# A fused FFT mixer and two MLPs: two blocks' MLP in halves by turns, fewer weight conversions in the first transform's columns, banks dealt by use

## The chip, the cores and the metric

The kernel runs on one core of a Trainium2 chip. The metric is the device time of one execution in microseconds, as the median of several runs. The kernel before took 1379.32 us (three runs, 1379.2 to 1383.39).

## What is computed

The input is x of shape 4 x 3136 x 256 (batch, sequence, channels). Three layers follow one another:

```python
X = np.fft.rfft(x, axis=1)
y = np.fft.irfft(X * (filt_r + 1j * filt_i), n=3136, axis=1)
h = y.transpose(0, 2, 1) @ U @ V
u = y + h.transpose(0, 2, 1)
u = u + np.maximum(u @ w_ch1, 0) @ w_ch2
xn = (u - mean(u)) / sqrt(var(u) + 1e-6) * g_ln
out = u + np.maximum(xn @ w_ch1b, 0) @ w_ch2b
```

The ranks and widths are 32 (U, V) and 1024 (both MLPs). U, V and the four weights arrive in 64-bit floating point and are converted on the chip; most products are made from two 32-bit pieces, a high and a low one.

## The kernel before, in words

**Head.** Batch 0's transform is done first and alone. `First.rows` (L431) multiplies the rows, `First.columns` (L500) works through 14 pairs of columns, numbered j = 0 to 13, with a tail of three more turns (`BACKL` = 3). One turn j of the columns does, for different columns at once: four transposes `psz` on TensorE (L538), their copy `z` on ACT (L546), the product `ps2` (L555) of the column before, the filter (`filt`, L218: two copies `psx` of crossed halves on ACT, the multiplications L228 and L231 on VectorE, the sum L232 on POOL), the product `ps3` (L564) of the column three turns back with a slot of `d` that holds the inverse matrix and that column's piece of U, and the copies of the result (`spill` L520, `project` L528). U's piece is copied into its slot by POOL (L574, L577), `UAHEAD` = 1 turn ahead. The PSUM pools are `ps_h` (three banks), `ps_o` (four) and `ps_t` (one). Before the change `psz` and both `ps3` share the four banks of `ps_o`, and the crossed halves of odd columns lie in `ps_t`.

**The converter.** `stagger` (L826) runs 18 jobs, each one piece of a weight or of V: job n starts at slot 4n, its two ACT conversions (L807, L808) come in that slot, then one VectorE instruction per slot (L794, L796, L798, L800), POOL's L812 and L814, the high piece (`keep`, mostly ACT) at slot 4n + 8 and the low piece (`last`, L885) in the next. Each `next(pr)` runs one slot. `ROWSLOTS` and `COLSLOTS` say how many slots go into which row and column; the main loop runs two slots per step until the jobs are done. A job's data are fetched to a staging tile some jobs ahead, by SP.

**Main loop.** The tokens lie in blocks of 512. A step (L1016) is one eighth of a block's MLP: the first product `psh` (`m1`, L663), ACT's and VectorE's halves `hh` and `hl` (L674, L675), and, two steps later, the second product `pso` (`m2`, L679). Phases are (a, k) for MLP 1 of block k and (b, k) for MLP 2, in the order a0 a1 a2 b0 b1 a3 b2 a4 b3 a5 and so on, eight steps each. `end` (L701) closes a phase: for MLP 1 it forms the tile `x2` (L712, L718, L721) and stores it (L750), for MLP 2 it adds and stores the output (L732, L742). A unit (L636) makes 448 tokens from the transform's last stage; its two loads (L628 and L634, `load_unit`) are issued on SP one unit ahead, and only if its batch's transform is complete. A block's units are due at steps 3 and 6 of the phase that `ahead` names. Batches 1 to 3 are transformed beside the loop by the generator `rest`: from step `FFT0` on, `RATE` pieces per step. `Spectrum.finish` (L273) completes a batch. All engines' queues run in the order in which the program is written.

Of the kernel before, what the change touches and what calls it, by code (L numbers as in the profile page):

```python
# [10 lines left out]
F32 = mybir.dt.float32  # L11
# [9 lines left out]
P = 128  # L21
PP, NM, NG = 112, 28, 28
KT, FT = D // P, FF // P
# [11 lines left out]
AHEAD = 3  # L35
FETCHES = (1, 2, 5, 6)

SLOTS, UAHEAD = 8, 1
PACE = 4
ROWSLOTS = (1, 2, 2, 2, 3, 3, 3, 4, 5, 5, 6, 6)  # L40
COLSLOTS = (0, 1, 1, 2, 2, 3, 3, 4, 4, 5, 5, 6, 6) + tuple(range(7, 14))
VSTEP = 9
DIRECT = 4

PARTS, UPARTS = (0, 1, 2, 5, 6, 8), 10
LEAD = 3
FFT0, RATE = 23, 0.75

XTURN, XREAD, XSTAT, XROOT = (3, 4), 8, (10, 11), 12
BW = 32  # L50
# [90 lines left out]
def fft_mixer_kernel(ctx: ExitStack, tc: tile.TileContext, x, U, V, flt, w1, w2, gln, w1b, w2b,  # L141
# [25 lines left out]
    def acopy(o, i, scale=1.0):  # L167
        nc.scalar.activation(out=o, in_=i, func=AF.Copy, scale=scale)  # L168
# [35 lines left out]
    def flat(t):  # L204
        return t.rearrange("p a d -> p (a d)")

    class Spectrum:
# [7 lines left out]
            nc.sync.dma_start(ft, flt[:, 2 * i:2 * i + 2])  # L215
            self.flt[i] = ft

        def filt(self, i, ps, room=None):  # L218
            ft = self.flt.pop(i)
            if room and i % 2:  # L220
                xs, ya = (mp.tile([P, BLK], F32, tag=tag, name=tag, bufs=3).rearrange("p (a d) -> p a d", a=2) for tag in ("hh", "hl"))
            else:
                xs = fp.tile([P, 2, D], F32, tag="xs", name="xs", bufs=2)
                ya = fp.tile([P, 2, D], F32, tag="ya", name="ya", bufs=3)
            crossed = room.tile([P, 512], F32, tag="t" if room is ps_t else "h", name="psx") if room else flat(xs)
            acopy(crossed[0:64], ps[64:128], -1.0)
            acopy(crossed[64:128], ps[0:64])
            nc.vector.tensor_tensor(out=ya, in0=ps.rearrange("p (a d) -> p a d", a=2), in1=ft[:, :, 0], op=ALU.mult)  # L228
            if room:
                def cross():  # L230
                    nc.vector.tensor_tensor(out=xs, in0=crossed.rearrange("p (a d) -> p a d", a=2), in1=ft[:, :, 1], op=ALU.mult)  # L231
                    (nc.gpsimd if i > 1 else nc.vector).tensor_tensor(out=ya, in0=ya, in1=xs, op=ALU.add)  # L232

                self.y[i] = ya, cross if i else cross()
                return
            nc.gpsimd.tensor_tensor(out=xs, in0=xs, in1=ft[:, :, 1], op=ALU.mult)  # L236
            self.y[i] = ya, xs
# [134 lines left out]
    class First:  # L372
# [127 lines left out]
        def columns(self):  # L500


            sp = Spectrum(0, self.flt)
            zt, n, w = {}, NCH, PP + R
            d0, d1 = self.d
            self.t = d1[:, 1, 0:KT * 2 * R].rearrange("p (h g r) -> p h g r", h=KT, g=2)
            turns = [self.u_half(h) for h in (1, 0)]

            def slot(g):
                return d1[:, 0] if g == 0 else d0[:, g % SLOTS]  # L510

            def total(j):
                if ADDL <= j < n + ADDL:
                    cross = sp.y[n - 1 - j + ADDL][1]
                    if cross:
                        cross()

            def spill(pvs, i):
                for dh, pv in enumerate(pvs):
                    (nc.vector.tensor_copy if dh else acopy)(self.big[:, dh, 2 * i * PP:2 * (i + 1) * PP].rearrange("p (g w) -> p g w", w=PP), pv[:, :, :PP])  # L520

            def project(pvs, i):
                for dh, pv in enumerate(pvs):
                    acc = self.t[:, dh]
                    if i == n - 1:
                        nc.vector.tensor_copy(acc, pv[:, :, PP:])
                    else:
                        nc.vector.tensor_tensor(out=acc, in0=pv[:, :, PP:], in1=acc, op=ALU.add)  # L528

            due = None  # L530
            for j in range(n + BACKL):
                if j < n:
                    i = n - 1 - j
                    ps = ps_o.tile([P, 512], F32, tag="o", name="psz")
                    for g in range(2):
                        for dh in range(KT):
                            a = g * D + dh * P
                            nc.tensor.transpose(ps[:PP, a:a + P], self.big[:, dh, (2 * i + g) * PP:(2 * i + g + 1) * PP], ident)  # L538
                total(j)
                if due:  # L540
                    spill(*due)
                    project(*due)
                due = None
                if j < n:
                    zt[i] = wide(F32, "fin", "z0", D, 3)
                    acopy(flat(zt[i]), ps[:PP])  # L546
                if 0 < j <= n:
                    i = n - j
                    z = zt.pop(i)
                    ps = ps_h.tile([P, 512], F32, tag="h", name="ps2")  # L550
                    if i == 0:
                        for g in range(2):
                            nc.tensor.matmul(ps[:, g * D:(g + 1) * D], self.e[:, 1 - g], z[:, g], start=True, stop=True)
                    else:
                        nc.tensor.matmul(ps, self.e[:, 0], flat(z), start=True, stop=True)  # L555
                    sp.filt(i, ps, ps_t if i % 2 else ps_h)
                if j >= BACKL:
                    i = n + BACKL - 1 - j
                    ya = sp.y.pop(i)[0]
                    pvs = []  # L560
                    for dh in range(KT):
                        ps = ps_o.tile([P, 512], F32, tag="o", name="ps3")
                        for g in range(2):
                            nc.tensor.matmul(ps[:, g * w:(g + 1) * w], dealt(ya[:, g], dh), slot(2 * i + g),  # L564
                                             start=True, stop=True)
                        pvs.append(ps[:, :2 * w].rearrange("p (g w) -> p g w", w=w))
                    due = pvs, i
                if j in UTURN:
                    next(turns[UTURN.index(j) // 2], None)
                self.filters(j + AHEAD)  # L570
                if BACKL - UAHEAD <= j < n + BACKL - UAHEAD:
                    i = n + BACKL - UAHEAD - 1 - j
                    for g in () if i else range(2):
                        nc.gpsimd.tensor_copy(slot(g)[:, PP:w], self.uf[:, g])  # L574
                    if i:
                        g = 2 * i % SLOTS
                        nc.gpsimd.tensor_copy(d0[:, g:g + 2, PP:w], self.uf[:, 2 * i:2 * i + 2])  # L577
                yield j
            project(*due)
            spill(*due)  # L580
# [120 lines left out]
    def end(ph):  # L701
# [1 line left out]
        n = blen(k)  # L703
        acc = po.pop(ph)
        if kind == "a":
            x2 = mp.tile([P, BLK // BW, BW, KT], F32, tag="x2", name="x2", bufs=1)

            def cut(t, dh):
                return t[k][:, dh, :n].rearrange("p (j c) -> p j c", c=BW)

            for dh in range(KT):
                nc.vector.tensor_tensor(out=x2[:, :n // BW, :, dh], in0=acc[dh][:, :n].rearrange("p (j c) -> p j c", c=BW),  # L712
                                        in1=f32(cut(acth, dh)), op=ALU.add)
            while len(todo) <= XROOT:
                todo.append([])
            for dh in range(KT):
                o, ah, al = x2[:, :n // BW, :, dh], cut(acth, dh), cut(actl, dh)
                todo[dh].append(lambda o=o, al=al: nc.vector.tensor_tensor(out=o, in0=o, in1=f32(al), op=ALU.add))  # L718
                todo[dh + 1].append(lambda o=o, ah=ah: acopy(ah, o))
                todo[dh + 2].append(lambda o=o, ah=ah, al=al: sub(al, o, f32(ah)))  # L720
                todo[XTURN[dh]].append(lambda o=o: nc.vector.transpose(out=o, in_=o))  # L721
            todo[XTURN[-1]].append(lambda: x2store(k, x2))
            todo[XREAD].append(lambda: x2load(k))
            for j, at in enumerate(XSTAT):
                todo[at].append(lambda j=j: x2stat(k, j))
            todo[XROOT].append(lambda: x2root(k))
            return
# [205 lines left out]
    with tc.manual_schedule():  # L933
# [6 lines left out]
        def chain():  # L940
# [2 lines left out]

        first = First()
        pr = stagger([w_job("w1", w1, 0, "wt"), w_job("w1", w1, 1, "wt"), v_job(0), v_job(1)] + [w_job(nm, w, j) for nm, w, j in (
            ("w2", w2, 0), ("w1", w1, 2), ("w1", w1, 3), ("w2", w2, 1), ("w2", w2, 2),
            ("w2", w2, 3), ("w1b", w1b, 0), ("w1b", w1b, 1), ("w2b", w2b, 0), ("w1b", w1b, 2), ("w1b", w1b, 3),
            ("w2b", w2b, 1), ("w2b", w2b, 2), ("w2b", w2b, 3))])
        first.load(pr)
# [62 lines left out]

        later = leftover()
        units_to(need(0))
        steps = [(ph, f) for ph in phases for f in range(FT)]
        for idx in range(len(steps) + 2):  # L1016
            if idx < len(steps):
                ph, f = steps[idx]
# [56 lines left out]
```

## Time and profile before

| what | value |
|---|---|
| median of three runs | 1379.32 us |
| the profiled execution | 1375.99 us |
| its span | 1374.2 us |
| mean granted TensorE clock | 0.999 |
| TensorE's slices 1 to 3 of 40, in tenths | 8, 7, 8 |
| TensorE's slices 4 to 39 | 9 |
| DMA, mean | 110 GB/s |

A slice is 34 us; 9 stands for 90% or more. "Idle before" in a row is the time in which the engine had nothing to run just before the instruction, with what ended it. Matmuls overlap, so their busy times can add up to more than the time that passes.

### The profile page before, as it was taken

Reading aid. Unit: us, or ns where it says so; the run is one execution under the profiler, and the core shown is the slowest. Engines: PE = TensorE matmul, PEld = TensorE weight load, DVE = VectorE, ACT = ScalarE, POOL = GpSimd, SP = SyncE. Lnnn points to the kernel's source line nnn. Section 1 sums busy time; section 2 is a strip of 40 time slices with the busy share of each in tenths; the row PEclk is TensorE's granted clock in tenths of the full one; section 3 lists DMA queues with packets and bytes.
Section 4 is the critical chain, followed back from the end, with each engine's and each line's share of the span. In section 5 each row is a group of like instructions: output and inputs, shape, how many; then the busy total and the mean of one; then the engine's idle time right before and its main releaser. Section 6 shows DMA issues by size and latency. Waiting matters only on the chain.

```text
span 1374.2 us, 18678 instructions
## 1 busy us (share of the span) xinstructions
PE 1342.1 (98%) x6870; PEld 1118.4 (81%) x6870; DVE 826.4 (60%) x1660; ACT 549.2 (40%) x1019; POOL 170.2 (12%) x173
## 2 busy tenths in 40 slices
PE   8789999999999999999999999999999999999998
PEld 7478788877888888888888888888888888888887
DVE  6878966577545546666555557675455445454554
ACT  4764544466333334554333335553222222222221
POOL 2846601022000001111000001110000000000000
PEclk9999999999999999999999999999999999999999
DMA  9735267474535534533345345443012112210111
GB/s 260 250 89 150 78 154 198 142 204 131 136 96 145 141 80 146 152 115 103 93 118 154 87 126 163 125 140 92 17 50 65 44 34 74 66 20 28 46 47 39
DMA packets 140155, 151.10 MB, mean 110 GB/s; under 512 B 60528, under 2 KB 116160, under 8 KB 139968
## 3 DMA queue, kind: packets, MB, share of 16 engines
q1 hardware_dynamic: 133600, 138.61, 36.1%
q0 software_dynamic: 5888, 10.50, 3.3%
q8 instruction: 54, 0.88, 0.3%
q10 hardware_dynamic: 576, 0.80, 0.2%
q14 instruction: 37, 0.30, 0.1%
HBM read 102.34 MB, written 47.54 MB: 109 GB/s over the span
## 4 chain that ended last, share of the span: by engine, by line
PE 86%; DVE 6%; ACT 2%; DMA 2%; issue 2%; POOL 1%; SPq 0%; DVEq 0%; ACTq 0%; POOLq 0%
PE psh L671 36%; PE pso L698 13%; PE pso L699 6%; PE pso L690 6%; PE pso L691 6%; PE pso L692 6%; PE psu L642 3%; PE ps L200 2%; PE ps L202 2%; PE ps L201 2%; DMA x<-x 1%; ACT xs L168 1%; PE psu L644 1%; DVE hl L675 1%; DVE x2t L732 1%
## 5 line engine op out<-in xcount | busy, mean ns | idle before, releaser
L675 DVE SCALAR_TENSOR_TENSOR hl<-psh,hh 128x512 fp32r<-128x512 f32 (+1 forms) x400 | 270.9, 678 | 411.9 <-ACT hh L674 411.5
L674 ACT ACTIVATE hh<-psh 128x512 fp32r<-128x512 f32 (+1 forms) x400 | 235.1, 588 | 624.8 <-PE psh L671 619.1
L698 PE MATMUL pso<-wb,hh 128*128 128x512 f32 x784 | 285.2, 397 | 0.9 <-DVE x L712 0.8
L671 PE MATMUL psh<-ah,wb 128*128 128x512 f32 (+1 forms) x800 | 276.7, 387 | 0.0
L699 PE MATMUL pso<-wb,hl 128*128 128x256 f32 x784 | 219.9, 280 | 0.6 <-DVE hl L675 0.6
L671 PEld LDWEIGHTS psh<-ah,wb 128*128 128x128 f32 x800 | 149.7, 188 | 33.3
L698 PEld LDWEIGHTS pso<-wb,hh 128*128 128x128 f32 x784 | 147.3, 188 | 35.2 <-DVE x L712 3.2
L690 PE MATMUL pso<-hh,w2h 128*128 128x512 f32 (+1 forms) x400 | 156.2, 390 | 1.0 <-DVE x2t L732 0.9
L691 PE MATMUL pso<-hl,w2h 128*128 128x512 f32 (+1 forms) x400 | 155.1, 388 | 1.6 <-DVE hl L675 1.4
L671 PE MATMUL psh<-ah,w1h 128*128 128x512 f32 (+1 forms) x400 | 155.5, 389 | 0.4 <-DVE hl L675 0.3
L671 PE MATMUL psh<-al,wb 128*128 128x512 f32 (+1 forms) x400 | 155.3, 388 | 0.0
L671 PE MATMUL psh<-al,w1h 128*128 128x512 f32 (+1 forms) x400 | 155.0, 387 | 0.0
L671 PE MATMUL psh<-ah,w1l 128*128 128x512 f32 (+1 forms) x400 | 154.6, 387 | 0.0
L692 PE MATMUL pso<-hh,w2l 128*128 128x512 f32 (+1 forms) x400 | 154.4, 386 | 0.0
L699 PEld LDWEIGHTS pso<-wb,hl 128*128 128x128 f32 x784 | 148.1, 189 | 6.9 <-DVE hl L675 1.2
L236 POOL TENSOR_TENSOR xs<-xs,ft 128x512 f32<-128x512 f32 x42 | 54.3, 1294 | 392.5 <-ACT xs L168 392.5
L690 PEld LDWEIGHTS pso<-hh,w2h 128*128 128x128 f32 x400 | 75.2, 188 | 19.2 <-issue 4.2
L691 PEld LDWEIGHTS pso<-hl,w2h 128*128 128x128 f32 x400 | 75.2, 188 | 17.4 <-DVE hl L675 3.7
L671 PEld LDWEIGHTS psh<-ah,w1h 128*128 128x128 f32 x400 | 75.2, 188 | 16.2 <-DVE hl L675 0.8
L671 PEld LDWEIGHTS psh<-ah,w1l 128*128 128x128 f32 x400 | 75.1, 188 | 15.8
L692 PEld LDWEIGHTS pso<-hh,w2l 128*128 128x128 f32 x400 | 75.1, 188 | 15.3
L671 PEld LDWEIGHTS psh<-al,w1h 128*128 128x128 f32 x400 | 75.3, 188 | 12.5 <-DVE al L171 0.2
(163 smaller groups left out, 1775.8 us busy)
## 6 DMA issues: line engine op xcount, KB each, us to landing
ft<-flt SPq DMA_DIRECT2D x42, 512.0 KB, 4.4
xd<-x SPq DMA_DIRECT2D x96, 128.0 KB, 2.9
x2t<-xd SPq DMA_DIRECT2D x24, 512.0 KB, 4.7
wt<-bd SPq DMA_DIRECT2D x24, 448.0 KB, 5.8
out<-x2t SPq DMA_DIRECT2D x84, 128.0 KB, 2.1
xt<-x SPq DMA_DIRECT2D x42, 224.0 KB, 3.7
zd<-ze SPq DMA_DIRECT2D x42, 224.0 KB, 2.7
zt<-zd SPq DMA_DIRECT2D x42, 224.0 KB, 3.5
```

The source lines that it names most:

```text
L200: nc.tensor.matmul(o, lh, rh, start=True, stop=False)
L201: nc.tensor.matmul(o, lh, rl, start=False, stop=False)
L236: nc.gpsimd.tensor_tensor(out=xs, in0=xs, in1=ft[:, :, 1], op=ALU.mult)
L642: nc.tensor.matmul(ps[:, m:UN:UW], t[:, m, dh * P:(dh + 1) * P], ic[:, m, :], start=m == 0, stop=False, skip_group_check=True)
L671: nc.tensor.matmul(ps[:, :n], w[:, kt, fs], a[:, kt, :n], start=j == 0, stop=j == 3 * KT - 1)
L674: nc.scalar.activation(out=hh[:, :n], in_=ps[:, :n], func=AF.Relu)
L675: nc.vector.scalar_tensor_tensor(out=hl[:, :n], in0=ps[:, :n], scalar=0.0, in1=f32(hh[:, :n]), op0=ALU.max, op1=ALU.subtract)
L690: nc.tensor.matmul(o, wh[:, f, ds], hh[:, :n], start=f == 0, stop=False)
L691: nc.tensor.matmul(o, wh[:, f, ds], hl[:, :n], start=False, stop=False)
L692: nc.tensor.matmul(o, wl[:, f, ds], hh[:, :n], start=False, stop=f == FT - 1)
L698: nc.tensor.matmul(o, hh[:, cs], w, start=f == 0, stop=False, skip_group_check=True)
L699: nc.tensor.matmul(o[:, D:], hl[:, cs], w[:, :D], start=False, stop=f == FT - 1, skip_group_check=True)
```

## The change

- **Converter.** 12 slots in the columns, one in each of columns 0 to 11, and not 20. w2's second piece is converted ahead of w1's second half.
- **Steps.** The first two phases are taken in halves by turns: a0's first four steps, a1's first four, a0's last four, a1's last four. Block 1's `x2` gets a buffer of the tag `x2t`.
- **Columns.** `psz` goes to `ps_t`, all crossed halves to `ps_h`; `ps_o` keeps `ps3`. Odd columns still use the tiles `hh` and `hl`. U's pieces are copied by ACT, two turns ahead. V is loaded at column 11, not 9.
- **Transform of the later batches.** `FFT0` goes from 23 to 25.

```diff
-SLOTS, UAHEAD = 8, 1
+SLOTS, UAHEAD = 8, 2
-COLSLOTS = (0, 1, 1, 2, 2, 3, 3, 4, 4, 5, 5, 6, 6) + tuple(range(7, 14))
-VSTEP = 9
+COLSLOTS = tuple(range(12))
+VSTEP = 11
-FFT0, RATE = 23, 0.75
+FFT0, RATE = 25, 0.75
...
-        def filt(self, i, ps, room=None):
+        def filt(self, i, ps, room=False):
...
-            crossed = room.tile([P, 512], F32, tag="t" if room is ps_t else "h", name="psx") if room else flat(xs)
+            crossed = ps_h.tile([P, 512], F32, tag="h", name="psx") if room else flat(xs)
...
-                    ps = ps_o.tile([P, 512], F32, tag="o", name="psz")
+                    ps = ps_t.tile([P, 512], F32, tag="t", name="psz")
...
-                    sp.filt(i, ps, ps_t if i % 2 else ps_h)
+                    sp.filt(i, ps, True)
...
-                        nc.gpsimd.tensor_copy(slot(g)[:, PP:w], self.uf[:, g])
+                        acopy(slot(g)[:, PP:w], self.uf[:, g])
...
-                        nc.gpsimd.tensor_copy(d0[:, g:g + 2, PP:w], self.uf[:, 2 * i:2 * i + 2])
+                        acopy(d0[:, g:g + 2, PP:w], self.uf[:, 2 * i:2 * i + 2])
...
-            x2 = mp.tile([P, BLK // BW, BW, KT], F32, tag="x2", name="x2", bufs=1)
+            x2 = mp.tile([P, BLK // BW, BW, KT], F32, tag="x2t", name="x2", bufs=2) if k == 1 else \
+                mp.tile([P, BLK // BW, BW, KT], F32, tag="x2", name="x2", bufs=1)
...
-            ("w2", w2, 0), ("w1", w1, 2), ("w1", w1, 3), ("w2", w2, 1), ("w2", w2, 2),
+            ("w2", w2, 0), ("w2", w2, 1), ("w1", w1, 2), ("w1", w1, 3), ("w2", w2, 2),
...
-        steps = [(ph, f) for ph in phases for f in range(FT)]
+        half = FT // 2
+        steps = [(ph, h * half + f) for h in range(2) for ph in phases[:2] for f in range(half)]
+        steps += [(ph, f) for ph in phases[2:] for f in range(FT)]
```

In the changed kernel lines from L707 to L1014 stand one further down (L794 is L795, L732 is L733).

The order of the instructions, first VectorE's in the columns, from the fourth column's first multiplication (`ya`, L228) to the fifth's and past it. Before:

```order
L228 TENSOR_TENSOR ya<-ps_563,f_427 128x512
L798 SCALAR_TENSOR_TENSOR ct<-stg,ct 128x512
L800 TENSOR_SCALAR cyh<-ct 128x512
L231 TENSOR_TENSOR xs<-psx,f_427 128x512
L520 COPY big<-ps_574 128x224
L528 TENSOR_TENSOR d_185<-ps_571,d_185 128x64
L528 TENSOR_TENSOR d_185<-ps_574,d_185 128x64
L228 TENSOR_TENSOR hl<-ps_606,f_456 128x512
L794 TENSOR_SCALAR cyh<-cyh 128x512
L796 TENSOR_SCALAR ct<-cyh 128x512
L231 TENSOR_TENSOR hh<-psx,f_456 128x512
```

And in the changed kernel, the same stretch:

```order
L228 TENSOR_TENSOR ya<-ps_545,f_427 128x512
L801 TENSOR_SCALAR cyh<-ct 128x512
L231 TENSOR_TENSOR xs<-psx,f_427 128x512
L520 COPY big<-ps_556 128x224
L528 TENSOR_TENSOR d_185<-ps_553,d_185 128x64
L528 TENSOR_TENSOR d_185<-ps_556,d_185 128x64
L228 TENSOR_TENSOR hl<-ps_587,f_456 128x512
L795 TENSOR_SCALAR cyh<-cyh 128x512
L231 TENSOR_TENSOR hh<-psx,f_456 128x512
```

Each column now holds one converting instruction, where the early ones held two.

Then SP's queue around the load of batch 1's first unit (`wt<-bd_116`; `bd<-be` are the transform's results, `xd<-x` the store of `x2`, `out<-x2t` block 3's output). Before:

```order
L271 DMA bd_116<-be 112x2x256 x4
L750 DMA xd_94<-x_3441 32x16x64 x4
L628 DMA ic<-c_inv 112x448
L634 DMA wt<-bd_116 112x1024
L742 DMA out<-x2t 32x4x256 x4
L297 DMA xt<-x 112x512 x2
```

And in the changed kernel:

```order
L751 DMA xd_94<-x_3409 32x16x64 x4
L271 DMA bd_116<-be 112x2x256 x2
L743 DMA out<-x2t 32x4x256 x4
L628 DMA ic<-c_inv 112x448
L634 DMA wt<-bd_116 112x1024
L757 DMA x2t<-xd_94 128x4x256
```

The unit's two loads, which stood ahead of the four output stores, stand behind them.

Last VectorE's queue at the same place (`tt` and `tk` are `finish`, `x2t` the eight updates of block 3's output). Before:

```order
L675 SCALAR_TENSOR_TENSOR hl<-psh,hh 128x512
L278 TENSOR_TENSOR tt<-pt,tt 32x256
L171 TENSOR_TENSOR tk<-tt,tk 32x256
L675 SCALAR_TENSOR_TENSOR hl<-psh,hh 128x512 x2
L732 SCALAR_TENSOR_TENSOR x2t<-pso,ln_3309,x2t 128x256 x8
```

And in the changed kernel:

```order
L171 TENSOR_TENSOR yl<-ya,yh 128x512
L675 SCALAR_TENSOR_TENSOR hl<-psh,hh 128x512 x2
L278 TENSOR_TENSOR tt<-pt,tt 32x256
L171 TENSOR_TENSOR tk<-tt,tk 32x256
L733 SCALAR_TENSOR_TENSOR x2t<-pso,ln_3241,x2t 128x256 x8
```

The two instructions of `finish` have moved two steps down, directly ahead of the updates that the stores wait for.

## Rows read from the trace of the kernel before

**Rows 1.** The page, part 1: busy us, share of the span, instructions.

```profile
PE 1342.1 (98%) x6870; PEld 1118.4 (81%) x6870; DVE 826.4 (60%) x1660; ACT 549.2 (40%) x1019; POOL 170.2 (12%) x173
```

**Rows 2.** Windows: stretch, busy time of each engine, clock, DMA share, GB/s.

```profile
31.60:85.90 54.30, 41.62 (x234) 28.82 (x233) 45.32 (x97) 37.36 (x74) 41.09 (x47) 0.97 0.70 216
...
120.00:183.00 63.00, 59.69 (x255) 45.29 (x255) 57.40 (x94) 28.27 (x51) 31.30 (x24) 1.00 0.39 102
```

**Rows 3.** Waits, 48.2 to 81.9 us: us in total, times, longest.

```profile
PE psz L538 <- DVE d L528: 3.4, 2, 2.4
```

**Rows 4.** Groups by line, VectorE, 48.2 to 81.9 us: busy us, mean ns.

```profile
L798 DVE SCALAR_TENSOR_TENSOR ct<-stg,ct 128x512 int32<-128x512 int32 x4 | 3.7, 935 | 0.0
L794 DVE TENSOR_SCALAR cyh<-cyh 128x512 f32<-128x512 f32 x3 | 3.6, 1191 | 0.0
L796 DVE TENSOR_SCALAR ct<-cyh 128x512 int32<-128x512 int32 x3 | 3.5, 1169 | 0.0
...
L800 DVE TENSOR_SCALAR cyh<-ct 128x512 int32<-128x512 int32 x3 | 1.3, 425 | 0.1
```

**Rows 5.** Timeline, VectorE, first columns: start us, us, instruction.

```profile
45.57 0.93 DVE L794 TENSOR_SCALAR cyh<-cyh 128x512 f32<-128x512 f32 x1
46.54 0.60 DVE L796 TENSOR_SCALAR ct<-cyh 128x512 int32<-128x512 int32 x1
```

**Rows 6.** Groups by line, ACT, 48.2 to 81.9 us; last number: idle before.

```profile
L168 ACT ACTIVATE big<-ps 128x224 f32<-128x224 f32 x11 | 3.8, 347 | 1.2 <-PE ps L564 1.1
...
L807 ACT ACTIVATE cyh<-stg 128x512 f32<-128x512 f32 x3 | 2.0, 664 | 0.9 <-ACT vh L168 0.9
```

**Rows 7.** The tile v_sb: first readers, its load, issue to landing.

```profile
L644 PE MATMUL psu<-v_sb,tk x56: 445/451/452, 89.8 to 1240.8; 96*128 96x448 f32 x56
L931 POOL DMA_DIRECT2D v_sb<-vd x1: 548/548/548, 67.5 to 67.5; - x1
...
DMA to landing us min/median/max: 9.9/9.9/9.9
```

**Rows 8.** Groups by line, VectorE, 131 to 180 us (main loop).

```profile
L794 DVE TENSOR_SCALAR cyh<-cyh 128x512 f32<-128x512 f32 x5 | 6.1, 1226 | 0.0
...
L796 DVE TENSOR_SCALAR ct<-cyh 128x512 int32<-128x512 int32 x5 | 4.3, 859 | 0.0
L798 DVE SCALAR_TENSOR_TENSOR ct<-stg,ct 128x512 int32<-128x512 int32 x5 | 3.4, 681 | 0.0
```

**Rows 9.** Timeline, VectorE and then TensorE, steps 26 to 28.

```profile
181.19 1.29 DVE L712 TENSOR_TENSOR x<-pso,ah 128x512 f32<-128x512 f32 x2 [2.39 <-DMA xd<-x]
...
188.81 0.69 DVE L675 SCALAR_TENSOR_TENSOR hl<-psh,hh 128x512 fp32r<-128x512 f32 x1 [1.70 <-ACT hh L674]
...
181.94 0.50 PE L698 MATMUL pso<-wb,hh 128*128 128x512 f32 x1 [0.79 <-DVE x L712]
```

**Rows 10.** Timeline at batch 1's first unit: SP, VectorE, TensorE; then line 634's landing.

```profile
355.18 0.63 SPq L634 DMA_DIRECT2D wt<-bd  x1
362.38 2.75 SPq L742 DMA_DIRECT2D out<-x2t  x4
...
355.53 0.40 DVE L278 TENSOR_TENSOR tt<-pt,tt 32x256 f32<-32x256 f32 x1
356.43 0.41 DVE L171 TENSOR_TENSOR tk<-tt,tk 32x256 fp32r<-32x256 f32 x1 [0.49 <-ACT tk L168]
...
366.71 1.04 PE L642 MATMUL psu<-ic,wt 112*128 112x112 f32 x8
...
DMA to landing us min/median/max: 3.9/5.8/9.8
```

**Rows 11.** Windows of 2 us in the columns, as in rows 2.

```profile
40.00:42.00 2.00, 0.54 (x4) 0.55 (x5) 1.97 (x4) 1.49 (x3) 1.55 (x3) 1.00 0.56 203
42.00:44.00 2.00, 2.00 (x10) 1.64 (x10) 0.86 (x2) 1.62 (x4) 2.00 (x2) 0.57 0.80 199
54.00:56.00 2.00, 0.23 (x2) 0.02 (x1) 1.97 (x3) 1.13 (x3) 1.82 (x2) 1.00 0.88 352
```

## The prediction

> **What bounds the kernel now.** I read the page first: TensorE is busy for 98% of the span and VectorE for 60% [rows 1]. A share like that is an average, so the table of windows comes next. Two stretches at the head stand out [rows 2]; elsewhere TensorE is so full that a change can only make it wait. They are the columns (31.6 to 85.9 us), with TensorE at 41.6 of 54.3 us and VectorE at 45.3, and the stretch of steps 8 to 26 of the main loop (120 to 183 us), with VectorE at 57.4 of 63. In the columns the waits name VectorE: the transposes of the next column waited 3.4 us for the additions that free their bank [rows 3]. So both stretches are paced by VectorE, which converts weights there besides its own work, and a conversion taken out of one comes back in the other.
>
> The page's span is 1374.2 us and the execution that it shows took 1375.99 us; the median of the runs is 1379.32, or 3.33 above. I make the sum against 1375.99 and add 3.33.
>
> **Fewer conversions in the columns.** The order shows what VectorE runs between two columns' first multiplications (L228). From the first column to the fourth there were six conversion instructions and are now three; an L800, an L794 and an L796 are gone, 0.43 + 0.93 + 0.60 = 1.9 us [rows 4, 5]. From the fourth to the last there were thirteen and are now eight: two L798, one L800, one L794, one L796 fewer, 2 x 0.94 + 0.43 + 1.19 + 1.17 = 4.7 us [rows 4]. VectorE paces this stretch, so all of it counts: -6.6 us. If another engine takes over the pace the gain is smaller, down to the 1.9 of the start; if the waits for banks [rows 3] go as well, 3.4 more. I take the middle, as the banks add nothing where VectorE itself is late.
>
> The banks: transposes get the single bank of ps_t, whose last reader is the copy of one column earlier; crossed halves share three banks with the spectra. Every new wait reaches back to work of the column before, so I cost them at 0; what hides them is a column's own 2 to 3 us, and without that cover the price is the 3.4 us again, the other way.
>
> U's copies leave POOL and go to ACT. ACT has none of that form; the nearest is its copy of 224 columns, 0.35 us [rows 6], so 10 columns cost it at most 3.5 us, and no less than nothing. In exchange the stretch loses one pair of ACT's conversions. I cost this at 0 while ACT is not the bound; it is the second rival. The copies stand two columns ahead of their use, so TensorE no longer waits for them. The load of V on POOL moves past two more columns: it was issued at 67.5 us, takes 9.9 to land and is first read at 89.8 [rows 7], so 12.4 us were spare; two columns of at most 3.4 us (from 48.2 to 81.9 us there are ten) leave 5.6, and I cost it at 0.
>
> **What comes back in the loop.** Eight slots of the converter are two weights' worth: two each of L794, L796, L798, L800, 2 x (1.23 + 0.86 + 0.68 + 0.43) = 6.4 us of VectorE [rows 4, 8]. The conversions go on for four steps more, up to step 26. There VectorE was idle for 2.39 and 1.70 us [rows 9], 4.1 us that can take them, which leaves 2.3. The 2.39 was a wait for the store of the tile x2, which held up TensorE by 0.79 us [rows 9]; with a tile of its own for block 1 that wait goes. Together +1.5 us. Bounds: -0.8, if all fits in idle time, and +6.4, if none does; I take the value that the idle rows give. Block 0's update of x2 now falls next to block 1's, which makes the clump denser, and this is why I don't go lower. ACT and POOL do their part of the two weights beside: ACT has 28.3 and POOL 31.3 of 63 us there, and their two staging loads meet a DMA share of 0.39 [rows 2].
>
> The halves by turns change no work on TensorE: the same 16 steps in another order, and one unit (block 2's last) earlier by four steps. w1's second half has its last pieces converted in steps 4 and 6 and is used from step 8.
>
> **The transform starts two steps later, and one load with it.** This term is as large as the columns'. FFT0 goes from 23 to 25, so batch 1's result is complete two steps later (step 73, not 71), while its first unit stays fixed at the end of step 75, because block 6 needs it. Its load may be issued only when the batch is complete. In the trace it was issued at 355.18 us, ahead of the four stores of block 3's output (362.38 us, taking 2.75), and the unit ran at 366.71 [rows 10]. In the new order it stands on SP **behind** those four stores, which wait for VectorE's eight updates. Ahead of these updates now stand also the two instructions that finish the batch, 0.40 + 0.49 + 0.41 = 1.3 us [rows 10]. So the stores end and the load is issued at 362.38 + 2.75 + 1.3 = 366.4. Such a load lands 3.9, 5.8 or 9.8 us after issue (least, median, most of 24) [rows 10]: 372.2 by the median, where TensorE wants it at 366.7. TensorE runs in order, and what is queued behind the unit is the whole loop: a wait of 5.5 us. Bounds 3.6 and 9.5. TensorE had no idle time there, so nothing hides it.
>
> A wait like that can cost more through the clock. In the trace, after two microseconds in which TensorE worked for 0.54, the granted clock was 0.57 for the next two, so mostly the lower level of 1.2 GHz: 0.9 us lost in that window; two microseconds with only 0.23 of work, at 54 to 56 us, left it at 1.00 [rows 11]. The rows allow both, 0 and 0.9. I take 0.9, because the gap of 5.5 us is longer than either. Wait and clock: +6.4 us.
>
> The Trainium skill ("TensorE: Matmul & The Clock Gate", section "Part 1: The HAM clock gate") says that the full clock is given for recent activity and that an idle engine falls back to half of it. By that rule the fall behind the wait is certain rather than possible. The rows at 42 us agree, those at 54 us show that not every gap does it; by the rule the sum is as above, without it 0.9 lower.
>
> **Sum:** -6.6 + 1.5 + 6.4 = +1.3 us; 1377.3 for a profiled execution, **1380.6** for the median. About 0.3%, or 4.1 us, is what a measurement of this kernel can tell from no change; 1.3 is below it.
>
> **Rivals.**
> - *The late load costs more than everything else gives (slower).* Place: the first unit of batch 1, at about 367 us. If the load takes the longest landing of the rows, the wait is 9.5 and with the clock 10.4: -6.6 + 1.5 + 10.4 = +5.3, 1384.6. It decides from a price of 9.2 on (6.6 - 1.5 + 4.1). For it: four stores and a smaller load are issued just ahead of it, and 5.8 is only the median. Against it: 9.8 is the worst of 24.
> - *ACT paces the columns (slower).* In two columns ACT has, on top of the column, a gap of 0.9 us while it issues V's stores and then the pair of conversions: 0.9 + 2 x 0.66 = 2.2 us [rows 6], 4.4 for both, and it has the copies of U too. Then the columns give 2.2 instead of 6.6: +5.7, 1385.0. Against it: the same clump stood in the columns before and VectorE, not ACT, was what TensorE waited for [rows 3].
> - *The load is in time (faster).* If the stores drain sooner or the load overtakes them, only the first two terms are left: -5.1, 1374.2. For it: batch 1 was ready early before. Against it: SP issues in order, and the stores stand ahead of it in the new order.
>
> **Numbers.** The forecast 0.50, the late load at its worst 0.23, ACT 0.12, the load in time 0.15. So faster by over 0.3% has 0.15, within it 0.50, slower 0.35. The range takes in the third rival with a microsecond below (1373) and reaches past the first two by four, because the loop term's own bound adds 4.9 (1389). The forecast alone, with its loop term between -0.8 and +4 and the rest as summed, is 1378.3 to 1383.1.
>
> **What would show it.** Right: the last column's L228 near 75 instead of 81.9 us; VectorE without a gap from about step 13 to 26, and no wait of L712's successor for a store; the load of batch 1's first unit issued behind the four stores, TensorE idle some 5 to 6 us ahead of that unit, and a granted clock under 1 behind it. Wrong: no idle time at that unit (then the time is near 1374); columns as long as before with ACT full; or the loop losing over 4 us to VectorE, which would break the second term.

## The result and the profile after

The changed kernel is slower. Its median is 1387.84 us over ten runs (1382.91 to 1391.36); the kernel before has 1377.03 in the runs beside it, a ratio of 1.0069 with a 95% interval of 1.0049 to 1.0088. The profiled execution took 1388.34 us, with a span of 1386.6. The time lies inside the predicted range, but the likeliest case (within 0.3%) did not come true.

Cut into stretches, the two spans show where it went. The boundaries are the first transpose `psz` of the columns, the first `psw` (end of the columns), and the first product `psh` of steps 0, 30, 72 and 80. Four of the kernels of the experiments are beside them, and each column of the table is one execution:

| stretch, us | before | changed | changed, FFT0 23 | before, FFT0 25 | changed, load on POOL | changed, FFT0 23, slots dealt otherwise |
|---|---|---|---|---|---|---|
| columns | 54.30 | 47.63 | 47.65 | 54.13 | 46.33 | 46.35 |
| to step 0 | 7.54 | 7.54 | 7.54 | 7.55 | 7.54 | 7.55 |
| steps 0 to 29 | 99.42 | 105.76 | 106.63 | 99.62 | 105.98 | 99.87 |
| steps 30 to 71 | 162.63 | 162.63 | 162.59 | 162.65 | 163.01 | 163.53 |
| steps 72 to 79 | 25.12 | 32.05 | 25.08 | 33.54 | 26.92 | 25.10 |
| step 80 to the end | 993.64 | 997.41 | 993.46 | 996.98 | 998.31 | 993.26 |

So -6.67 in the columns, +6.34 in steps 0 to 29, +6.93 at batch 1's first unit and +3.77 after it: +10.37. The other 2 us of the difference between the spans are in the start: the first `psz` began at 31.55 us in the one execution and at 33.58 in the other. In all the profiles it began between 31.55 and 34.73 us, though the programs are the same up to there.

The page's part 1 of the changed kernel, which answers to [rows 1]: TensorE's work is the same 6870 instructions.

```profile
PE 1348.6 (97%) x6870; PEld 1123.5 (81%) x6870; DVE 822.7 (59%) x1660; ACT 550.8 (40%) x1034; POOL 165.7 (12%) x158
```

Its windows, with the columns of [rows 2]: first the columns, then steps 9 to 26, step 12, the second centering, and three at batch 1's first unit.

```profile
33.58:81.21 47.63, 40.33 (x233) 28.69 (x233) 34.76 (x89) 34.98 (x82) 26.62 (x24) 0.96 0.68 214
...
120.00:183.00 63.00, 57.21 (x223) 43.84 (x222) 56.33 (x85) 27.78 (x48) 38.57 (x27) 0.92 0.39 106
...
133.00:137.00 4.00, 3.86 (x10) 3.10 (x11) 2.39 (x5) 0.69 (x1) 3.06 (x3) 0.57 0.40 131
...
164.00:168.00 4.00, 2.68 (x5) 1.49 (x5) 3.71 (x8) 0.93 (x2) 2.11 (x2) 0.50 0.54 185
...
372.00:374.00 2.00, 0.00 (x0) 0.00 (x0) 0.00 (x0) 0.00 (x0) 0.00 (x0) 1.00 0.96 310
374.00:376.00 2.00, 1.61 (x11) 1.56 (x12) 0.00 (x0) 0.01 (x1) 0.00 (x0) 0.85 1.11 341
376.00:378.00 2.00, 2.00 (x10) 1.96 (x10) 0.62 (x1) 0.53 (x1) 0.00 (x0) 0.50 1.03 268
```

VectorE has 10.6 us less to do in the columns than before (34.76 against 45.32, [rows 2]), and ACT is now as full as it is. In the main loop the granted clock of the 63 us fell from 1.00 to 0.92, so some 10 us of them (63 x 0.08 / 0.5) ran at the lower level of 1.2 GHz: they lie at step 12 and at the second centering. Behind the wait at the unit the clock was 0.50 again.

The groups of the converter on VectorE, from the fourth column's L228 to the last (48.5 to 77.3 us), which answer to [rows 4]:

```profile
L799 DVE SCALAR_TENSOR_TENSOR ct<-stg,ct 128x512 int32<-128x512 int32 x2 | 1.7, 835 | 0.0
L795 DVE TENSOR_SCALAR cyh<-cyh 128x512 f32<-128x512 f32 x2 | 1.4, 690 | 0.0
L797 DVE TENSOR_SCALAR ct<-cyh 128x512 int32<-128x512 int32 x2 | 1.2, 590 | 0.0
```

With L801's two they are eight instructions for thirteen, as the order said, but the first passes are also shorter: 690 and 590 ns for 1191 and 1169. POOL is busy for 26.6 us in the columns and was for 41.1. The Trainium skill ("SBUF — State Buffer", section "Who interferes with whom") says that VectorE and GpSimd contend for one shared pair of ports, as a lock. The shorter passes agree with it, but it is not shown here. Experiment 3 keeps the conversions of the kernel before and has POOL busy for 35.3 us only: over its columns these two passes took 740 and 875 ns for 1127 and 1026 before, and those of L798 1198 for 935.

TensorE's longest waits of the whole run: us in total, times, longest.

```profile
PE pso L690 <- DVE x2t L733: 5.8, 5, 1.3
PE psz L538 <- ACT z L168: 4.1, 4, 1.6
PE psu L642 <- DMA wt<-bd: 3.3, 1, 3.3
PE pso L692 <- POOL w2l L886: 2.4, 1, 2.4
PE psw L895 <- DVE hl L675: 1.9, 1, 1.9
...
PE psw L895 <- DVE wg L876: 1.3, 1, 1.3
```

The second row lies in the columns, the last three in the loop (at steps 12 and 21), the third at batch 1's first unit, and the first is spread over the run.

The timeline at that unit, SP, VectorE and TensorE, which answers to [rows 10]:

```profile
366.63 2.75 SPq L743 DMA_DIRECT2D out<-x2t  x4
369.47 0.54 SPq L628 DMA_DIRECT2D ic<-c_inv  x1
370.11 0.39 SPq L634 DMA_DIRECT2D wt<-bd  x1
...
364.00 0.40 DVE L278 TENSOR_TENSOR tt<-pt,tt 32x256 f32<-32x256 f32 x1
364.89 0.41 DVE L171 TENSOR_TENSOR tk<-tt,tk 32x256 fp32r<-32x256 f32 x1 [0.49 <-ACT tk L168]
365.33 3.23 DVE L733 SCALAR_TENSOR_TENSOR x2t<-pso,ln,x2t 128x256 f32<-128x256 f32 x8
...
366.75 0.47 PE L690 MATMUL pso<-hh,w2h 128*128 128x512 f32 x1 [1.32 <-DVE x2t L733]
374.39 1.16 PE L642 MATMUL psu<-ic,wt 112*128 112x112 f32 x8 [3.31 <-DMA wt<-bd]
```

Two instructions of `finish` stand ahead of the eight updates, the updates ahead of the four stores, and the stores ahead of the load. TensorE first waits 1.32 us for a bank that the updates free, then 3.31 for the load.

### The profile page after: what moved, and what is told of

It is laid out like the page before. It is cut to its first block, busy times and chain, and to the rows that moved or that the text cites. A ratio compares the mean times of both kernels' runs of the same rounds, so it can differ in the third digit from the quotient of the medians.

```text
span 1386.6 us, 18686 instructions
## 1 busy us (share of the span) xinstructions
PE 1348.6 (97%) x6870; PEld 1123.5 (81%) x6870; DVE 822.7 (59%) x1660; ACT 550.8 (40%) x1034; POOL 165.7 (12%) x158
## 4 chain that ended last, share of the span: by engine, by line
PE 83%; DVE 7%; DMA 3%; ACT 3%; issue 2%; POOL 1%; SPq 1%; ACTq 0%; DVEq 0%; POOLq 0%
PE psh L671 35%; PE pso L698 12%; PE pso L699 6%; PE pso L690 6%; PE pso L692 6%; PE pso L691 6%; PE psu L642 3%; PE ps L200 2%; PE ps L202 2%; PE ps L201 2%; DMA x2t<-xd 2%; DVE x2t L733 1%; ACT xs L168 1%; PE psu L644 1%; DVE hl L675 1%
```

## The experiments

**1 and 2. FFT0 alone, both ways.** The changed kernel with 23, and the kernel before with 25.

```diff
-FFT0, RATE = 25, 0.75
+FFT0, RATE = 23, 0.75
```

> The changed kernel with FFT0 back at 23: batch 1 is complete two steps sooner and its first unit's load stands ahead of block 3's stores again. Theory (the late load is the largest loss, and the shift by two steps costs more further on): the wait of 3.31 us at step 75 and the low clock behind it go, 7.7 us at that place, and the some 3.6 us that the changed kernel loses after 420 us go too; what stays is the columns' gain of 4.6 and the loop's loss of 6.3, so 1.7 over the kernel before: a ratio of 1.001 (0.999 to 1.003). Rival (the load is late because the loop ahead of it ran late, and FFT0 only moved it): 1.005 or more, with the wait for wt<-bd still there.

> The kernel before with FFT0 = 25 and nothing else. Theory: it alone costs what it costs in the changed kernel, 7.7 us at step 75 and up to 3.6 further on: a ratio of 1.006 to 1.008, with TensorE idle 3 us or more for wt<-bd ahead of batch 1's first unit. Rival (it needs the loop's delay to do harm): 1.000 to 1.002.

Measured: 1375.69 us, ratio 0.9988 (0.9976 to 0.9999), and 1388.91 us, ratio 1.0084 (1.0068 to 1.0099). The mechanism holds in both directions; the ratios lie just outside what was expected (0.9988 for at least 0.999, 1.0084 for at most 1.008). The one constant is worth some 12 us in the changed kernel (1387.84 less 1375.69) and 11.9 in the kernel before. It needs nothing of the loop's delay. With 23 the load is issued ahead of the stores again, as the timeline of SP shows:

```profile
355.88 0.65 SPq L634 DMA_DIRECT2D wt<-bd  x1
363.10 2.75 SPq L743 DMA_DIRECT2D out<-x2t  x4
```

**3. The columns' banks and ACT's copies alone**, in the kernel before.

```diff
-SLOTS, UAHEAD = 8, 1
+SLOTS, UAHEAD = 8, 2
...
-                    ps = ps_o.tile([P, 512], F32, tag="o", name="psz")
+                    ps = ps_t.tile([P, 512], F32, tag="t", name="psz")
...
-                        nc.gpsimd.tensor_copy(d0[:, g:g + 2, PP:w], self.uf[:, 2 * i:2 * i + 2])
+                        acopy(d0[:, g:g + 2, PP:w], self.uf[:, 2 * i:2 * i + 2])
```

> The kernel before with the columns' part alone that is not the converter: psz in ps_t, crossed halves in ps_h, U's copies on ACT two turns ahead. Theory (the banks cost nothing and save nothing, since VectorE paces the columns): the first step starts within 1 us of the kernel before, ratio 0.9993 to 1.0007. Rival 1 (the single bank of the transposes and ACT's copies cost what the columns fell short of the forecast): the first step is 1.5 to 2.5 us later, ratio 1.001 to 1.002. Rival 2 (the waits for the bank go): up to 3.4 us earlier, ratio 0.9975.

Measured: 1377.04 us, ratio 0.9998 (0.9986 to 1.0011). The first step came 1.9 us later than before, which reads like rival 1, but the columns began 2.9 us later in that execution; they took 53.31 us for 54.30. So the banks and copies cost nothing and save next to nothing, as expected, and a step's place in the span says nothing before the start of the head is taken off. The reason given for it (VectorE paces the columns) holds only in part. TensorE's waits over the whole of the columns in the kernel before:

```profile
PE ps L564 <- POOL d L577: 4.9, 5, 2.3
PE psz L538 <- DVE d L528: 3.4, 2, 2.4
```

And in this one:

```profile
PE ps L564 <- POOL hl L232: 3.9, 5, 1.5
...
PE ps L564 <- POOL ya L232: 1.7, 3, 0.9
```

The longest wait before was for U's copies on POOL; with the copies on ACT it became a wait for POOL's sums, 5.6 us.

**4. Two more slots in the columns** (14, with FFT0 23).

```diff
-COLSLOTS = tuple(range(12))
+COLSLOTS = tuple(range(14))
```

> The changed kernel with FFT0 = 23 and two more converter slots in the columns (one in each of 14, for 12), so that every conversion in the loop comes one step sooner. Theory (the loop lost its 6.3 us to two late conversions and the low clock behind them, w2's last low piece on POOL at step 12 the first): the wait of 2.44 us at step 12 goes, the columns give about 1 us less, and the time is 1 to 3 us under the same kernel with 12 slots, ratio 0.998 to 1.000. Rival (the loop loses because VectorE has too much to do there, whatever the slot): within 1 us of the kernel with 12 slots, with the idle time only moved.

Measured: 1376.99 us, ratio 1.0005 (0.9991 to 1.0018). The wait at step 12 went and steps 0 to 29 took 102.74 us for 106.63, but the columns took 49.73 for 47.65; and the second centering still waited 1.31 and 2.00 us, with the clock at 0.50 behind. Neither expectation holds whole: the one late piece is cured by an earlier slot, the centering is not, and the gain in the loop goes back in the columns.

**5. One step less: FFT0 = 24.**

> The changed kernel with FFT0 = 24: batch 1 is complete one step sooner, and its first unit's load stands ahead of block 3's four stores instead of behind them. Theory (it is the place in SP's queue, not the step, that costs): the wait for wt<-bd at step 75 is gone as with 23; the ratio to the kernel before is 0.998 to 1.002. Rival (each step of delay costs, wherever the load stands): half of the difference between 23 and 25, 1.003 to 1.005, with a wait for wt<-bd of 1 us or more.

Measured: 1378.56 us, ratio 1.001 (0.9997 to 1.0024). The wait for the load is gone: steps 72 to 79 take 24.36 us. So at the unit it is the place in SP's queue that decides, and not the step. But from step 80 on the rival has a share: 995.24 us, between 993.46 (23) and 997.41 (25), so 1.8 us for the first step and 2.2 for the second.

**6. The unit's two loads on POOL's queue**, with FFT0 = 25.

```diff
+        queue = nc.gpsimd if i == UPB else nc.sync
-        wt[i] = new_unit(i)
-        nc.sync.dma_start(wt[i][0], bd[b].rearrange("(q m) w -> q m w", m=NM)[:, m0:m0 + UW, :])
+        wt[i] = new_unit(i, queue)
+        queue.dma_start(wt[i][0], bd[b].rearrange("(q m) w -> q m w", m=NM)[:, m0:m0 + UW, :])
```

> The changed kernel (FFT0 = 25) with one thing else: the two loads of batch 1's first unit are issued by POOL, whose queue has no stores in it, at the same place in the program. Theory (the load is late because SP issues it behind four stores that wait for VectorE's updates): it is issued before 365 us and not at 370, the wait of 3.31 us goes and with it the half clock behind it, 4 to 6 us in all; the waits for the updates (L733) stay; ratio 1.002 to 1.005. Rival (the batch itself is complete too late, whatever the queue): the unit still waits 2 us or more for wt<-bd; 1.006 or more.

Measured: 1381.12 us, ratio 1.0027 (1.0011 to 1.0043); steps 72 to 79 took 26.92 us for 32.05. Timeline of POOL, SP and TensorE (lines are one further down):

```profile
360.55 0.54 POOL L635 DMA_DIRECT2D wt<-bd  x1 [9.56 <-DMA bd<-be]
...
364.27 2.75 SPq L744 DMA_DIRECT2D out<-x2t  x4
...
364.39 0.47 PE L691 MATMUL pso<-hh,w2h 128*128 128x512 f32 x1 [1.32 <-DVE x2t L734]
368.58 1.04 PE L643 MATMUL psu<-ic,wt 112*128 112x112 f32 x8
```

The batch was complete early enough: the load goes out 3.7 us ahead of the stores, as soon as `bd` has landed, and the unit waits for nothing. That is the theory, with the 1.32 us for the updates left over, as expected. The Trainium skill ("Perfetto Trace Analysis", section "DMA Optimizations") advises to give inputs and outputs to different issuing engines; this run agrees, with 5.1 us for one load.

**7. The transform's piece behind the updates**, with FFT0 = 25.

```diff
+                        turn = True
+                        if not ending:
+                            next(rest, None)
...
                     end(steps[idx - 2][0])
+                    if turn and ending:
+                        next(rest, None)
```

> The changed kernel (FFT0 = 25) with one thing else: in a step that ends a block of MLP 2, the transform's piece is issued behind the block's eight updates and not ahead of them. Theory (after 420 us the loss comes from the transform's VectorE work standing ahead of those updates, for which the next block's first product waits 1.3 us at a time): the waits for x2t L733 fall from 5.8 us to about 1 and the time by 4 to 7 us with what the clock loses less; ratio 1.001 to 1.004. Rival (VectorE is as busy either way and the wait moves to the transform's own products): within 2 us of the changed kernel, 1.005 to 1.008.

Measured: 1385.96 us, ratio 1.0063 (1.0048 to 1.0077), so the rival. The waits of this kernel, in which L733 no longer appears:

```profile
PE psh L671 <- ACT be L168: 5.2, 3, 1.8
...
PE psu L642 <- DMA wt<-bd: 3.3, 1, 3.3
```

The five waits for the updates became three for ACT's copies of the transform, and step 80 to the end took 997.07 us for 997.41. My theory of the loss after step 80, that the order of these two on VectorE makes it, falls. (Steps 0 to 29, where the program is that of the changed kernel, took 104.36 us for 105.76: after the same wait at step 12 the clock stayed at 1.00 in this execution.)

**8 to 10. The converter's slots in the loop dealt otherwise**, all with FFT0 = 23: a third slot in some early steps, one instead of two in steps 14 to 21. The first version has the third slot in steps 0 to 5, the second has none, the third in steps 5, 6, 8 and 9:

```diff
                 next(pr, None)
+                if idx in (5, 6, 8, 9):
+                    next(pr, None)
...
-                next(pr, None)
+                if not 14 <= idx < 22:
+                    next(pr, None)
```

> The changed kernel with FFT0 = 23 and the converter's slots in the loop dealt otherwise: three per step in steps 0 to 5, where VectorE has idle time, one per step in steps 14 to 21, where it has none. Theory (in steps 12 to 22 the loop is paced by VectorE, which two blocks' ends and the conversions fill together): the waits of 2.44 us at step 12 and of 1.94 and 1.09 us at the second centering shrink to under 1 us each, the clock stays at 1.00, and the loop from step 0 to step 30 takes 100 to 103 us, not 106.6; ratio 0.994 to 0.998. Rival (each of the two waits is a single late instruction, and VectorE's load in between plays no part): the waits move to other steps and the loop stays over 105 us; ratio 0.998 to 1.000.

Measured: 1371.56 us, ratio 0.9959 (0.9944 to 0.9974). Steps 0 to 29 took 101.11 us; between 116 and 176 us the timeline lists no wait of TensorE, at a clock of 1.00. The theory holds, with 4.7 us paid back in steps 0 to 11 (44.71 for 40.04).

> The changed kernel with FFT0 = 23 and one converter slot per step in steps 14 to 21, without the extra slots of steps 0 to 5. Theory (the second centering waits because VectorE is behind, so fewer conversions ahead of it are enough there; the wait at step 12 is another one and needs the pieces sooner): the waits at the second centering fall from 3.0 us to under 1, the wait of 2.44 us at step 12 for w2's low piece stays, steps 2 to 8 cost nothing more; step 0 to step 30 takes 99 to 103 us; ratio 0.993 to 0.997. Rival (the gain came from the extra slots): step 0 to step 30 over 104 us, ratio over 0.997.

Measured: 1374.84 us, ratio 0.9983 (0.9975 to 0.9992); 103.32 us. The waits at the centering are gone and that at step 12 stayed, as expected, but steps 0 to 29 and the ratio miss the theory's limits by little: conversions that were held back came late for block 0's MLP 2 (the wait for `wb`). The ratio is on the rival's side and cannot be told from that of experiment 1 (0.9976 to 0.9999), so fewer slots at the centering, without the earlier ones, gain nothing that is clear of the noise. The waits of this kernel, over the whole run:

```profile
PE pso L698 <- DVE wb L886: 2.5, 1, 2.5
PE pso L692 <- POOL w2l L886: 2.4, 1, 2.4
...
PE pso L698 <- DVE x L713: 1.4, 1, 1.4
```

The first and the last lie in steps 26 to 30, the middle one at step 12.

> As the version with the slots dealt otherwise, but with the extra slots in steps 5, 6, 8 and 9 in place of 0 to 5. Theory (the extra slots cost 4.9 us in steps 2 to 7 because they met the first units, whose copies VectorE makes): that loss shrinks to under 2 us, the wait at step 12 and those at the second centering stay away, and step 0 to step 30 takes 97 to 100 us; ratio 0.992 to 0.995. Rival (a conversion costs the same wherever it is put): 101 us as before, ratio 0.996.

Measured: 1370.82 us, ratio 0.9966 (0.995 to 0.9981); 99.87 us, and 40.14 in steps 0 to 11. The early loss is gone and steps 0 to 29 are as expected, but the ratio misses (0.9966 for at most 0.995): two waits of 2.3 us came in, at the first centering and for L713, and the time is that of the first version within the intervals. Windows of this version over 68 us of the loop and at its first centering:

```profile
112.00:180.00 68.00, 63.16 (x281) 50.24 (x280) 63.30 (x101) 33.26 (x59) 38.99 (x31) 1.00 0.46 126
...
132.00:136.00 4.00, 1.83 (x6) 1.22 (x7) 3.41 (x7) 1.16 (x2) 2.99 (x2) 1.00 0.42 131
136.00:140.00 4.00, 4.00 (x19) 3.30 (x19) 4.00 (x8) 3.11 (x6) 2.74 (x2) 1.00 0.00 0
```

The same of experiment 1, with its second centering:

```profile
112.00:180.00 68.00, 62.38 (x253) 48.02 (x252) 59.97 (x89) 30.36 (x53) 39.43 (x29) 0.92 0.42 114
...
160.00:164.00 4.00, 1.60 (x3) 0.46 (x3) 4.00 (x8) 2.70 (x5) 0.37 (x1) 0.75 0.57 99
164.00:168.00 4.00, 4.00 (x8) 2.48 (x9) 3.71 (x8) 1.23 (x2) 3.66 (x3) 0.50 0.78 263
168.00:172.00 4.00, 4.00 (x18) 3.23 (x17) 3.33 (x6) 1.83 (x4) 1.07 (x2) 0.90 0.01 2
```

In the same time this version's VectorE did 3.3 us more work and its TensorE 28 matmuls more.

**11. The same dealing in the kernel before**, four steps earlier.

> The kernel before with its converter slots dealt in the same way (three per step in steps 5, 6, 8, 9, one in steps 10 to 17, as its slots run four steps ahead). Theory (the columns' gain of the change is real and the dealing only keeps the loop from giving it back): the kernel before has 1.9 us of such waits (0.25 and 1.42 at its second centering, 0.24 and more elsewhere) and gains at most 1 to 3 us: ratio 0.998 to 0.9995. Rival (the dealing alone makes the time, and the change adds nothing): 0.996 or less.

Measured: 1381.15 us, ratio 1.0035 (1.0024 to 1.0045): slower, outside both expectations. Its conversions, already earlier by eight slots, met other work at other steps (waits of 2.1 to 2.3 us at 127, 142 and 183 us), and steps 0 to 29 took 104.83 us for 99.42. So this dealing is no gain by itself. What experiment 10 has over the kernel before is in the columns (46.35 us for 54.30); its steps 0 to 29 are level (99.87 for 99.42).

## Why the prediction was right in its range and wrong in its sum

- **Columns, -6.6: right in size, with a reason that holds only in part.** They took 6.67 us less; in all eight kernels with these columns they took 46.3 to 47.7 us. The step "VectorE paces this stretch, so all of it counts" failed. VectorE saved 10.6 us and not 6.6, as its remaining conversions were shorter too, and not all of that counted. It was busy for 45.32 of 54.30 us before, and TensorE waited longer for POOL's copies of U (4.9 us) than for VectorE (4.5 in all); [rows 3] begins at 48.2 us and shows VectorE's row alone. The prediction saw that this wait for POOL would end and put that at nothing. With the copies off POOL TensorE waited 5.6 us for POOL's sums (experiment 3); with eight slots' conversions gone as well that fell to 0.5, and ACT's copies `z` came first, with 4.1. POOL's work fell by 14.5 us (41.1 to 26.6), and how much of the 6.67 is VectorE's and how much POOL's no run separates, so that the sum hit the size is partly luck. The last L228 came at 77.24 us, which is 75.2 with the later start taken off (forecast 75). Banks and U's copies cost nothing on balance, as costed (experiment 3).
- **Loop, +1.5: wrong, +6.3.** The failed step is "4.1 us that can take them". That idle time lies in steps 26 to 28, behind the second centering. TensorE stopped where VectorE fell behind, at step 21 (1.94 and 1.32 us, for one wait of 1.42 before), and what is idle later can't pay for it. The sum also put ACT's and POOL's part of the conversions at nothing: w2's last low piece, a single late POOL instruction, held TensorE up for 2.44 us at step 12. The wait of L713's product, which I took as gone, was 1.07 us for 0.79; it was no longer for the store, but for VectorE's other work. These waits are 4.6 us longer than those before, and the clock, which had no term in the loop, was at its lower level for some 10 us. The two overlap, and how the 6.3 divides between them was not measured. My upper bound (+6.4, none fits) was near the time, but as the price of VectorE's work alone. The experiments show it from the other side. With the step-12 wait gone (experiment 4) the loop takes 3.9 us less; with the same work dealt otherwise over the steps, 5.5, 3.3 and 6.8 us come back (experiments 8 to 10). In the medians 8 and 10 are 4.1 and 4.9 us below experiment 1, and 9 only 0.9.
- **The late load, +6.4: right in mechanism**, +6.93, **and in size by errors that cancel.** The wait was 3.31 us and not 5.5: the load landed 4.3 us after issue, for a median of 5.8 that I had taken, and the unit was wanted 1.0 us behind the issue and not 0.3, as TensorE had just waited 1.32 us for the updates. That second wait, for updates that stand behind `finish`, was not in the sum. The clock of 0.50 behind the load cost some 1.8 (5.1 us that experiment 6 gives back, less 3.31) and not 0.9; the three make 6.4 of the 6.93. [rows 11] priced the clock with two microseconds, but in the same trace the next two are as slow, with TensorE busy throughout:

```profile
44.00:46.00 2.00, 2.00 (x7) 1.30 (x6) 1.29 (x4) 0.30 (x1) 2.00 (x4) 0.57 0.93 301
```

The Trainium skill ("TensorE: Matmul & The Clock Gate", section "Part 1: The HAM clock gate"), by which an idle engine falls to half the clock, agrees at this place; after the wait of 1.32 us at 641 us the windows stay at 1.00.
- **Not in the sum: +3.8 from step 80 on.** I moved one batch and FFT0 moves three. The pieces of batches 2 and 3 fall on other steps too; the changed kernel waits twice for 1.3 us there, at 641 and 907 us, where the transform's L228 stands ahead of the updates, and once for 0.5. That is 3.1 us against 0.9 with 23; two more waits, for the halves `hl` (0.36 and 0.43 us at 545 and 861 us), are not there with 23 either. But experiment 7 took the waits for the updates away and the time stayed, so the order by itself is not the cause. What makes the +3.8 is open; it comes with FFT0 (experiments 1, 2 and 5), and which step a piece has to avoid was only tried by FFT0 itself.
- **The rivals.** "Slower" came true, though not by the worst landing, which its mechanism wanted, but by the loop's term, which was too small, and by the one that was not in the sum. Sum by the measured terms: -6.67 + 6.34 + 6.93 + 3.77 = +10.37, against +1.3. The time stayed within the range because its upper end added the loop's own bound to the worst landing.

## What to carry to other kernels

Idle time of an engine counts only ahead of the point where its work is wanted; before putting work into a gap, look whether the engine that waits gets there first. Read the waits over the whole of a stretch before naming the engine that paces it: a window that starts late can leave out the longest. A constant that delays a generator delays everything that it makes: follow each of its products to the queue in which it is next issued, not the nearest one alone. A load that stands behind stores inherits what the stores wait for; another issuing queue, or one step sooner, frees it.

## What the runs showed of the hardware

- Equal gaps did not treat TensorE's clock alike. Around and after the waits of 1.94 and 1.09 us of experiment 1 the windows show 0.75, 0.50 and 0.90 in turn; after one of 2.29 us in experiment 10 the clock stayed at 1.00. (Windows under experiment 10.) Even the same wait at the same place did not: after the 2.44 us at step 12 the clock fell in the changed kernel (0.57 over the 4 us from 133 us) and in experiments 1, 5 and 6, and stayed at 1.00 in experiments 7 and 9, whose programs are the same up to there. Experiment 9:

```profile
132.00:136.00 4.00, 3.52 (x15) 2.92 (x16) 2.96 (x6) 1.28 (x2) 3.06 (x3) 1.00 0.42 128
```

In steps 0 to 29 of one program that made some 1.4 us (104.36 for 105.76, experiment 7).

- Executions differ most in the head: the first `psz` began between 31.55 and 34.73 us, and the same columns took 46.3 to 47.7, while the stretch from the columns' end to step 0 took 7.54 to 7.56 us in twelve of thirteen kernels. A table of stretches therefore tells more than the times of two executions do, down to the 1.4 us that the clock made.
